# Block attention and two dense layers on one core: token regions ahead of weight forms in SBUF, one attention step on another engine, longer planned zero products, a new order

## The chip, the core and the metric

The kernel runs on one core of a Trainium2 chip. The metric is device time in microseconds (us). Engines: PE (TensorE, matmuls), PEld (its weight loads), DVE (VectorE), ACT (ScalarE), POOL (GpSimd), SP (SyncE, which issues the transfers). Each takes its instructions in the order of the program, and semaphores tie the engines together.

## The reference

Attention inside chunks of 64 tokens (4 batches, 8 heads, 576 tokens, head size 64), then two dense layers on the 2304 x 512 result:

```
scores = scale * (q_c @ k_c.T)            # per chunk of 64
scores = scores - max(scores)
attn = exp(scores) / (sum(exp(scores)) + 1e-09)
x = (attn @ v_c) as 2304 x 512
x = (s * relu(x @ w_in)**2 + b) @ w_out           # 512 -> 2048 -> 512
x = (softplus(x @ moe2_w_in)) @ moe2_w_out        # 512 -> 2048 -> 512
```

All data is float32.

## The kernel before

**Numbers in halves.** Float32 operands are cut into two fp32r parts, `hi` (ACT casts it, L616) and `lo` (DVE subtracts, L625), and each product is three matmuls: hi·hi, hi·lo, lo·hi. The weights come as 64-bit words from DRAM and are turned into floats on the chip by `convert`: per tile of 128x512 DVE runs L483, L499, L514 and L583, and ACT one or two activations.

**Products.** The first matrix of each layer is multiplied by Winograd's form of Strassen's scheme: `quad(ph, i, j)` makes seven products (`p1` to `p7`) for a block of weights `i` (8 of them) and a group of tokens `j` (3 of them), so 24 quads a layer. A product is six matmuls of 128 x 384 columns (two inner halves by three part products, L1073). The products accumulate on one another in PSUM: `p1` is copied by ACT to a second bank (a seed, L1095), `p6` adds to the first, ACT or DVE takes a copy (L438 or L440), `p7` adds again, ACT seeds a third bank and DVE subtracts (L603), and so on. So five or six products of a quad wait for an ACT or DVE instruction that itself waits for an earlier product of the same quad. Other quads' products stand between as the order has them. The second matrix (`second_by_blocks`, matmuls at L1362) runs over 21 steps a layer, each of 8 x 6 matmuls.

**Attention.** Nine units `u` of 256 tokens each. For each: scores on PE (L847), a maximum by DVE (L868, `tensor_reduce`), and for half of the heads (`EARLY`) the maximum times -1/8 by DVE (L891, `tensor_scalar`), eight exponentials by ACT with it as the bias (L879); the other half has its maximum subtracted by DVE (L924) and one exponential (L937). Sums, reciprocals (L957 ACT, L960 DVE), the scaling by POOL (L964), transposes (L978), values (L1005), then the seven Strassen forms of the tokens as hi and lo (`block_forms`).

**Order.** Each step is an `Op` with candidate engines, a key and its dependencies. `Work.order` lays all 3907 of them out by a list schedule over estimated costs; the keys decide among those that are ready, and `TUNE` is a table of offsets to the keys. So the order on each engine is a result of `TUNE` and of the ops' engines. `Work.warmed` then fills the planned idle time of PE in the attention part with zero products (128 x 512 matmuls of zeros into bank S2, L1566), as many as fit by the cost that it plans for one.

**Place in SBUF.** One pool hands out SBUF in the order in which tiles are made: `operands` (two buffers of Strassen weight forms), `mem` (raw weights, sums, staging), small tiles, and then the six `region` tiles (token forms), at their first use. In every quad the weights stand in `operands` and the tokens in two regions. In the second matrices the tokens are hi and lo pieces in region 4 (layer one) or 0 (layer two), and the weights stand in `operands` too, with two exceptions: forms 4 to 7 of layer one stand in regions 1 and 2 (4 x 3 steps of 48 matmuls, 576), and the last eighth of the other steps stands higher up in the tokens' own region (10 x 3 x 6, 180). So of the 4032 matmuls of products 3276 have their weights in `operands` and 756 in a region.

Of the kernel before, what the change touches and what calls it, by code (L numbers as in the profile page):

```python
# [8 lines left out]
F32 = mybir.dt.float32  # L9
F32R = mybir.dt.float32r  # L10
# [3 lines left out]
ALU = mybir.AluOpType  # L14
# [4 lines left out]
P = 128  # L19
# [10 lines left out]
SCALE = 1.0 / float(D) ** 0.5  # L30
# [46 lines left out]

REGION = GROUP * XS // 2
TYPED = {(r, v) for r in range(2 * NG) for v in (1, 3)} | {(1, 2), (2, 2), (4, 2), (0, 4)}
AT_FORMS2 = 0  # L80
LATE = 4
AT_RAWS = 2048, 3 * REGION
# [8 lines left out]
SUMS_BY = ["POOL"] * 2 + ["DVE"] * 6  # L91

TUNE = {
# [36 lines left out]
}  # L130


# [18 lines left out]
class Work:  # L151
# [11 lines left out]
    BYTES = 330e3  # L163

    COLD = 7.0

    def __init__(self):
        self.ops = []
# [103 lines left out]

    def warmed(self, done, emit, kind, index):

        t, out, unused = 0.0, [], True
        for op in done:
            unused = unused and all((u.kind, u.index) != (kind, index) for u in op.takes)
            if op.on == "PE" and unused:
                for x in range(int((op.start - t) / self.IDLE / (2 if op.start < self.COLD else 1))):
                    out.append(Op({"PE": self.IDLE}, 0, [], [], [], emit, 0))  # L280
                    out[-1].on, out[-1].start = "PE", t + x * self.IDLE
                    out[-1].end = out[-1].start + self.IDLE
                t = op.end
            out.append(op)
        return out
# [20 lines left out]
def block_attention_two_layers(  # L306
# [36 lines left out]
    nc = tc and tc.nc  # L343
    work = Work()

    if tc:
        const = ctx.enter_context(tc.tile_pool(name="const", bufs=1))
        dram = ctx.enter_context(tc.tile_pool(name="dram", bufs=1, space=DRAM))
        pp = ctx.enter_context(tc.tile_pool(name="psum", bufs=1, space=PSUM))
        operands = const.tile([P, AT_WF - AT_W1], F32R, name="operands")  # L350
        shared = {}
        plain = const.tile([P, WORDS - AT_WF], F32, name="mem")
        bank = {
            kind: [pp.tile([P, 512], F32, name=f"{kind}{i}") for i in range(n)]
            for kind, n in (("A", 2), ("S", 3), ("at", 3))
        }
        ident = const.tile([P, P], F32, name="ident")
        nought = const.tile([P, P], F32R, name="nought")
        minus = minus_r = None
        s_sb = const.tile([P, 1], F32, name="s_sb")  # L360
        b_sb = const.tile([P, 1], F32, name="b_sb")
        small = [
            [const.tile([P, 2 * H], F32, name=f"{x}{i}") for x in ("mx", "sm")]
            for i in range(2)
        ]
        summed = {
            (ph, n, j): dram.tile([P, NF, N], F32, name=f"summed{ph}_{n}_{j}")
            for ph in range(2)
            for n in range(1, 8)
            for j in range(NG)  # L370
        }
        forms2 = [dram.tile([P, 7, NF, 256], F32, name=f"forms2_{ph}") for ph in range(2)]
        bias = const.tile([P, KK], F32, name="bias")
        unit = const.tile([P, 8], F32, name="unit")
# [415 lines left out]
    held = {}  # L790
# [10 lines left out]
    def attention(u, key):  # L801
# [56 lines left out]
        mx, sm = small[u % 2] if tc else (None,) * 2  # L858
        heads = lambda x: x.rearrange("p (h k) -> p h k", k=D)
        copied = []  # L860
        for hp in range(2):
            sc, pt = scores_in[hp], Place("at")
            h = slice(hp * H, (hp + 1) * H)
# [5 lines left out]
                    out=mx[:, h], in_=heads(at(sc)), op=ALU.max, axis=AX.X  # L869
# [4 lines left out]
            if (u, hp) in EARLY:  # L874

                def exps(e, sc=sc, hp=hp):
                    for y in range(H):
# [8 lines left out]
                        )  # L886

                o3 = add(
                    {"DVE": 0.08},
                    key,  # L890
                    lambda e, h=h: nc.vector.tensor_scalar(  # L891
                        out=mx[:, h], in0=mx[:, h], scalar1=-SCALE, scalar2=None, op0=ALU.mult
                    ),
                    [o2],
                )
                o5 = add({"ACT": 8 * 0.3}, key, exps, [o3], [sc], w=es)
            elif (u, hp) in BY_PE:

                def shift(e, sc=sc, h=h):
# [14 lines left out]
                        out=of("e", hp), in_=at(sc), func=AF.Exp, scale=SCALE  # L914
# [5 lines left out]
            else:  # L920
# [4 lines left out]
                        out=heads(of("e", hp)),  # L925
                        in0=heads(at(sc)),
                        in1=mx[:, h].unsqueeze(2).to_broadcast([P, H, D]),
                        op=ALU.subtract,
# [9 lines left out]
                        out=of("e", hp), in_=of("e", hp), func=AF.Exp, scale=SCALE  # L938
# [4 lines left out]
            if (u, hp) not in EARLY:  # L943
# [3 lines left out]
                    lambda e, h=h, hp=hp: nc.vector.tensor_reduce(  # L947
                        out=sm[:, h], in_=heads(of("e", hp)), op=ALU.add, axis=AX.X
                    ),
                    [o4],  # L950
                    r=es,
# [5 lines left out]
                lambda e, h=h: nc.scalar.activation(out=sm[:, h], in_=sm[:, h], func=AF.Identity, bias=1e-9),  # L957
# [10 lines left out]
                    op=ALU.mult,  # L968
# [667 lines left out]
```

## Time and profile before

| | |
|---|---|
| runs | 815.45 us median of three (812.33 to 816.46) |
| the profiled execution | 815.57 us, of which 813.8 us is the span from the first to the last instruction |
| PE busy | 785.0 us, 96% |
| DVE, ACT, POOL busy | 688.1, 551.2, 151.9 us |
| transfers | 214.94 MB, mean 264 GB/s |
| granted TensorE clock | 0.994 of full on the mean |

The stages, from the timeline: attention mixed with the first quads to about 105 us, the other quads of layer one to about 280 us, its second matrix to about 450 us, the quads of layer two to about 632 us, its second matrix to the end. The page's slices are 20.3 us wide; PE is at "9" or close to it nearly everywhere, so what matters is how many matmuls a stretch holds and what the short gaps wait for.

### The profile page before, as it was taken

To read this page: it belongs to the slowest core of one execution; us is meant where nothing else is said; L and a number is where in the kernel's file an instruction comes from. 1 tells how busy PE (TensorE), PEld (TensorE's weight loads), DVE (VectorE), ACT (ScalarE), POOL (GpSimd) and SP (SyncE) were. 2 spreads that over 40 slices of the span, in tenths; PEclk is the share of its full clock that TensorE was granted. 3 is DMA by queue.
4 is the path that set the end of the run, shared out by engine and by line. 5 is a ranking of instruction groups with operands and counts; after the bars stand their busy time and mean duration, and the time that the engine had idled before them with its cause. 6 is when DMAs were issued, how large, how long until landed. Compare 5 with 4: busy or idle time off the path is not lost.

```text
span 813.8 us, 15584 instructions
## 1 busy us (share of the span) xinstructions
PE 785.0 (96%) x5374; PEld 758.0 (93%) x5374; DVE 688.1 (85%) x1318; ACT 551.2 (68%) x1241; POOL 151.9 (19%) x146
## 2 busy tenths in 40 slices
PE   9998989899899899999999999999999999999998
PEld 6777889899899799999999899999999999999998
DVE  5989877998997779999999899999965867777865
ACT  4678977878987856778687756566555656555543
POOL 1677545121210004000022340121210000000000
PEclk9998999999999999999999999999999999999999
DMA  8656368989989997999862167989979987678851
GB/s 305 215 178 213 116 208 293 316 302 320 358 279 343 360 330 275 351 360 349 291 222 79 39 217 265 309 295 317 331 254 331 314 328 238 226 238 284 284 175 59
DMA packets 99279, 214.94 MB, mean 264 GB/s; under 512 B 10368, under 2 KB 71040, under 8 KB 97664
## 3 DMA queue, kind: packets, MB, share of 16 engines
q1 hardware_dynamic: 99200, 213.95, 76.7%
q8 instruction: 42, 0.69, 0.4%
q14 instruction: 37, 0.30, 0.1%
HBM read 128.45 MB, written 85.46 MB: 263 GB/s over the span
## 4 chain that ended last, share of the span: by engine, by line
PE 58%; DVE 8%; ACT 3%; DMA 2%; issue 1%; POOL 0%; ACTq 0%
PE S L1362 15%; PE at L1362 15%; PE at L1073 11%; PE A L1362 10%; PE S L1073 5%; PE A L1073 3%; DVE mem L603 2%; DVE region L625 2%; DMA summed<-mem 2%; ACT region L616 1%; DVE operands L625 1%; DVE mem L569 0%; DVE mem L514 0%; ACT mem L1105 0%; ACT S L1095 0%
## 5 line engine op out<-in xcount | busy, mean ns | idle before, releaser
L1073 PE MATMUL at<-region,operands 128*128 128x384 f32 x960 | 186.4, 340 | 5.7 <-ACT S L1095 4.6
L603 POOL TENSOR_TENSOR mem<-mem 128x256 f32<-128x256 f32 (+1 forms) x109 | 111.5, 1034 | 390.2 <-DVE mem L583 304.3
L1073 PEld LDWEIGHTS at<-region,operands 128*128 128x128 f32 x960 | 168.9, 188 | 10.6 <-ACT S L1095 8.2
L616 ACT CAST region<-mem 128x384 fp32r<-128x384 f32 (+3 forms) x210 | 110.1, 533 | 71.7 <-PE at L1362 44.8
L625 DVE TENSOR_TENSOR region<-mem,region 128x384 fp32r<-128x384 f32 (+2 forms) x204 | 112.5, 564 | 34.9 <-ACT region L616 33.7
L616 ACT CAST region<-region 128x384 fp32r<-128x384 f32 (+3 forms) x206 | 104.7, 521 | 53.5 <-PE at L1362 38.7
L625 DVE TENSOR_TENSOR region<-region,region 128x384 fp32r<-128x384 f32 (+3 forms) x206 | 113.9, 571 | 23.8 <-ACT region L616 22.5
L603 DVE TENSOR_TENSOR mem<-mem 128x384 f32<-128x384 f32 (+1 forms) x237 | 126.7, 556 | 7.7 <-ACT mem L1105 3.1
L1073 PE MATMUL S<-region,operands 128*128 128x384 f32 x624 | 127.0, 342 | 3.5 <-ACT S L1095 2.9
L1073 PEld LDWEIGHTS S<-region,operands 128*128 128x128 f32 x624 | 111.6, 190 | 6.0 <-ACT S L1095 4.2
L1362 PE MATMUL S<-region,operands 128*128 128x384 f32 (+1 forms) x504 | 116.2, 338 | 0.4 <-DVE region L625 0.4
L1362 PE MATMUL at<-region,operands 128*128 128x384 f32 (+1 forms) x504 | 115.7, 338 | 0.0
L1073 PE MATMUL A<-region,operands 128*128 128x384 f32 x432 | 90.4, 348 | 5.3 <-DVE A L603 2.5
L1362 PEld LDWEIGHTS S<-region,operands 128*128 128x128 f32 x504 | 90.5, 188 | 0.7 <-DVE region L625 0.7
L1362 PEld LDWEIGHTS at<-region,operands 128*128 128x128 f32 x504 | 90.7, 188 | 0.0
L1073 PEld LDWEIGHTS A<-region,operands 128*128 128x128 f32 x432 | 76.9, 191 | 8.4 <-DVE A L603 4.4
L1105 ACT ACTIVATE mem<-S 128x384 f32<-128x384 f32 x104 | 50.6, 490 | 26.2 <-PE S L1073 9.9
L625 DVE TENSOR_TENSOR operands<-mem,operands 128x768 fp32r<-128x768 f32 (+2 forms) x56 | 56.7, 1018 | 2.0 <-ACT operands L616 1.2
L1095 ACT COPY S<-at 128x384 f32<-128x384 f32 x80 | 37.9, 474 | 22.5 <-PE at L1073 19.8
L1116 ACT ACTIVATE mem<-mem 128x384 f32<-128x384 f32 x96 | 49.0, 529 | 1.1
L616 ACT CAST operands<-mem 128x768 fp32r<-128x768 f32 (+2 forms) x56 | 46.2, 834 | 4.7 <-POOL mem L603 3.0
L1362 PE MATMUL S<-region,region 128*128 128x384 f32 x192 | 45.1, 338 | 2.7 <-ACT region L616 1.9
(103 smaller groups left out, 1068.3 us busy)
## 6 DMA issues: line engine op xcount, KB each, us to landing
summed<-mem SPq DMA_DIRECT2D x336, 192.0 KB, 4.2
region<-summed SPq DMA_DIRECT2D x44, 768.0 KB, 5.9
mem<-in_w_dram SPq DMA_DIRECT2D x64, 512.0 KB, 5.2
mem<-summed SPq DMA_DIRECT2D x40, 768.0 KB, 5.0
forms<-mem SPq DMA_DIRECT2D x12, 512.0 KB, 5.3
region<-forms SPq DMA_DIRECT2D x6, 1024.0 KB, 8.4
mem<-forms SPq DMA_DIRECT2D x6, 1024.0 KB, 7.3
region<-in_q_dram SPq DMA_DIRECT2D x18, 256.0 KB, 4.0
```

What stands on the lines that cost most here:

```text
L603: lambda e: on(e).tensor_tensor(out=out(), in0=x(), in1=y(), op=op or ALU.subtract),
L616: lambda e: nc.scalar.copy(out=hi().bitcast(F32R), in_=x()),
L625: lambda e: on(e).tensor_tensor(out=lo().bitcast(F32R), in0=x(), in1=hi(), op=ALU.subtract),
L1073: nc.tensor.matmul(acc(dst)().rearrange("p (u c) -> p u c", u=GROUP), l[a], r[c], start=start and kk == 0 and x == 0, stop=kk == 1 and x == 2,
L1095: lambda e: nc.scalar.copy(out=acc(place)(), in_=acc(ba)()),
L1105: lambda e: nc.scalar.activation(out=at(go), in_=acc(place)(), func=AF.Softplus if ph else AF.Relu),
L1116: lambda e: nc.scalar.activation(out=at(go), in_=at(go), func=AF.Square),
L1362: nc.tensor.matmul(at(accs[d])[:, : N if c else N + more], l[a], r[c], start=i == 0 and y == 0, stop=i == NF - 1 and y == 2,)
```

## The change

Four edits: the six region tiles are made before all others; the negated maximum is made by ACT in place of DVE; `warmed` starts its zero products at 4.2 us of the plan and gives one that begins before 8 us 1.9 times the usual cost (before: from 0, twice the cost if the op after them starts before 7 us); and `TUNE` is another table, which moves instructions on every engine.

```
+FIRST_USES = [(0, 1), (1, 1), (2, 1), (3, 1), (4, 0), (5, 0)]
...
 TUNE = {
-    "attention 0": -425.5, "attention 0/0": -645, "attention 0/16": 5, "attention 1": -590.5,
+    "attention 0": -366, "attention 1": -248, "attention 1/25": 22.5, "attention 1/28": -18,
...
+    FIRST = 4.2
...
-        t, out, unused = 0.0, [], True
+        t, out, unused = self.FIRST, [], True
...
-                for x in range(int((op.start - t) / self.IDLE / (2 if op.start < self.COLD else 1))):
+                while True:
+                    cost = self.IDLE * (1.9 if t < self.COLD + 1 else 1)
+                    if t + cost > op.start:
+                        break
...
+        shared = {
+            (r, v): const.tile([P, REGION], F32R if (r, v) in TYPED else F32, name=f"region{r}_{v}", tag=f"region{r}")
+            for r, v in FIRST_USES
+        }
         operands = const.tile([P, AT_WF - AT_W1], F32R, name="operands")
-        shared = {}
...
-                    {"DVE": 0.08},
+                    {"ACT": 0.12},
                     key,
-                    lambda e, h=h: nc.vector.tensor_scalar(
-                        out=mx[:, h], in0=mx[:, h], scalar1=-SCALE, scalar2=None, op0=ALU.mult
-                    ),
+                    lambda e, h=h: nc.scalar.mul(out=mx[:, h], in_=mx[:, h], mul=-SCALE),
```

Where the tiles lie in each partition, in bytes, as the two built programs have it:

| tile | before | after |
|---|---|---|
| six regions, 21504 each | 99328 to 228352 | 16512 to 145536 |
| `operands`, 28672 | 16512 | 145536 |
| `mem`, 52736 | 45184 | 174208 |

Counted over the whole order, the zero products (L1566 before, L1577 after) are 113 before and 109 after. Of the 144 products of each layer that wait for an ACT or DVE step on their own quad, the number with no other PE step or just one between the product that is read and the one that waits was 33 in layer one and 40 in layer two; now it is 24 and 33. With none between: 4 and 1; now 0 and 2.

DVE at the start of the program. `mx` holds maxima, `sm` sums, `mem` the raw weights of the first block, `at` are PSUM banks with scores. Before:

```order
L868 TENSOR_REDUCE mx_77<-at_70 128x8
L499 TENSOR_SCALAR mem<-mem 128x512
L891 TENSOR_SCALAR mx_77<-mx_77 128x8
L868 TENSOR_REDUCE mx_77<-at_71 128x8
L514 SCALAR_TENSOR_TENSOR mem<-mem 128x512
L924 TENSOR_TENSOR region_0_143<-at_71,mx_77 128x512
```

And now:

```order
L496 TENSOR_SCALAR mem<-mem 128x512
L512 TENSOR_SCALAR mem<-mem 128x512
L527 SCALAR_TENSOR_TENSOR mem<-mem 128x512
L512 TENSOR_SCALAR mem<-mem 128x512
L496 TENSOR_SCALAR mem<-mem 128x512
L527 SCALAR_TENSOR_TENSOR mem<-mem 128x512
L596 SCALAR_TENSOR_TENSOR mem<-mem 128x512 x2
L881 TENSOR_REDUCE mx_83<-at_76 128x8
L881 TENSOR_REDUCE mx_83<-at_77 128x8
```

The eight steps of the first block's conversion have moved ahead of the first maximum (on SP the two transfers that bring it now stand ahead of the first four of q and k, too), and the negation of `mx` is gone from DVE.

On PE, late in the attention part, the end of quad (1, 1) of layer one. Each row is the first of the five that make up a product. Before, `A1` is the bank that the products accumulate in and `S2`, `S0` are the seeded banks:

```order
L1073 MATMUL S1_68<-region2_1_796,operands_63 128x384
...
L1073 MATMUL A1_66<-region2_1_796,operands_63 128x384
...
L1073 MATMUL S2_69<-region2_1_796,operands_63 128x384
...
L1073 MATMUL A1_66<-region2_1_796,operands_63 128x384
...
L1073 MATMUL S0_67<-region2_1_796,operands_63 128x384
```

And now, where `A0` and `S1` belong to quad (0, 1):

```order
L1084 MATMUL A1_72<-region2_1_65,operands_69 128x384
...
L1084 MATMUL S2_75<-region2_1_65,operands_69 128x384
...
L1084 MATMUL A0_71<-region2_1_65,operands_69 128x384
...
L1084 MATMUL S1_74<-region2_1_65,operands_69 128x384
...
L1084 MATMUL S0_73<-region2_1_65,operands_69 128x384
...
L1084 MATMUL A1_72<-region2_1_65,operands_69 128x384
```

Before, the product on a seeded bank follows directly on the `A1` product whose result the seed or the subtraction takes; now three products stand between the first such pair.

## Rows read from the trace of the kernel before

**Rows 1.** The page: span, and busy time of each engine.

```profile
span 813.8 us, 15584 instructions
PE 785.0 (96%) x5374; PEld 758.0 (93%) x5374; DVE 688.1 (85%) x1318; ACT 551.2 (68%) x1241; POOL 151.9 (19%) x146
```

**Rows 2.** Four stretches: length, busy PE, PEld, DVE, ACT, POOL, then PEclk, DMA, GB/s.

```profile
60.00:80.00 20.00, 17.11 (x311) 15.26 (x310) 18.06 (x36) 17.02 (x65) 15.41 (x14) 0.83 0.70 238
100.00:120.00 20.00, 16.50 (x82) 15.53 (x81) 15.76 (x25) 14.11 (x31) 10.27 (x10) 0.91 0.60 202
120.00:280.00 160.00, 150.96 (x831) 144.45 (x830) 137.71 (x266) 131.44 (x279) 29.79 (x29) 1.00 0.94 322
620.00:780.00 160.00, 160.00 (x913) 160.00 (x912) 118.88 (x224) 93.33 (x188) 0.00 (x0) 1.00 0.82 278
```

**Rows 3.** Waits of PE's weight loads, 120 to 640 us: total, times, longest.

```profile
PEld at L1073 <- ACT S L1095: 8.2, 11, 2.5
PEld A L1073 <- DVE A L603: 4.4, 5, 2.0
PEld S L1073 <- ACT S L1095: 3.1, 3, 1.5
```

**Rows 4.** Timeline, 0 to 10 us: start, length, engine, line, operation.

```profile
2.59 0.91 SPq L446 DMA_DIRECT2D mem<-in_w_dram  x2
4.24 3.97 PE L1566 MATMUL S<-nought 128*128 128x512 f32 x9
8.15 0.69 PE L847 MATMUL at<-region 64*64 64x64 f32 x32
9.95 0.69 DVE L868 TENSOR_REDUCE mx<-at 128x8 f32<-128x512 f32 x1 [7.92 <-PE at L847]
```

**Rows 5.** DMA issues: bytes and median time to landing.

```profile
mem<-in_w_dram SPq DMA_DIRECT2D x64, 512.0 KB, 5.2
```

**Rows 6.** Groups of DVE's instructions by line: busy, mean ns, idle before.

```profile
L514 DVE SCALAR_TENSOR_TENSOR mem<-mem 128x512 f32<-128x512 uint32 x56 | 38.5, 698 | 0.1
L483 DVE TENSOR_SCALAR mem<-mem 128x512 int32<-128x512 int32 x64 | 27.6, 432 | 6.5 <-DMA mem<-in_w_dram 6.5
L891 DVE TENSOR_SCALAR mx<-mx 128x8 f32<-128x8 f32 x9 | 8.1, 895 | 0.0
```

**Rows 7.** Line L891: shortest, median, longest in ns; and who waited.

```profile
L891 DVE TENSOR_SCALAR mx<-mx x9: 161/755/2152, 10.9 to 84.8; 128x8 f32<-128x8 f32 x9
  ACT region L879: 18.4, 7
```

**Rows 8.** Timeline, 66 to 76 us: POOL, DVE and PE around one L891.

```profile
66.95 2.59 POOL L625 TENSOR_TENSOR region<-mem,region 128x1024 fp32r<-128x1024 f32 x1 [0.40 <-ACT region L616]
68.40 1.17 DVE L891 TENSOR_SCALAR mx<-mx 128x8 f32<-128x8 f32 x1
72.14 0.33 PE L847 MATMUL at<-region 64*64 64x64 f32 x2 [0.76 <-ACT region L879]
```

**Rows 9.** Line L957, ACT on a tile of the same size: shortest, median, longest.

```profile
L957 ACT ACTIVATE sm<-sm x18: 205/253/294, 14.0 to 89.5; 128x8 f32<-128x8 f32 x18
```

**Rows 10.** Zero products, group of PE's instructions: busy, mean ns.

```profile
L1566 PE MATMUL S<-nought 128*128 128x512 f32 x113 | 32.5, 425 | 0.0
```

**Rows 11.** Groups of matmuls, 372 to 398 us: busy, mean ns, idle.

```profile
L1362 PE MATMUL at<-region,region 128*128 128x384 f32 x66 | 15.0, 334 | 0.0
```

**Rows 12.** The same, 690 to 716 us.

```profile
L1362 PE MATMUL at<-region,operands 128*128 128x384 f32 x45 | 10.5, 337 | 0.0
```

**Rows 13.** The chain that ended last, pieces of 48 matmuls: start, length.

```profile
367.12 8.32 PE A L1362 x48
658.68 8.43 PE A L1362 x48
```

**Rows 14.** Two groups of matmuls by their operands, whole span.

```profile
L1073 PE MATMUL at<-region,operands 128*128 128x384 f32 x960 | 186.4, 340 | 5.7 <-ACT S L1095 4.6 <-ACT mem L438 1.0
L1362 PE MATMUL at<-region,operands 128*128 128x384 f32 (+1 forms) x504 | 115.7, 338 | 0.0
```

More of the change, by code (lines that the diff above doesn't have):

```diff
@@ L278, in warmed @@
             if op.on == "PE" and unused:
-                for x in range(int((op.start - t) / self.IDLE / (2 if op.start < self.COLD else 1))):
+                while True:
+                    cost = self.IDLE * (1.9 if t < self.COLD + 1 else 1)
+                    if t + cost > op.start:
+                        break
                     out.append(Op({"PE": self.IDLE}, 0, [], [], [], emit, 0))
-                    out[-1].on, out[-1].start = "PE", t + x * self.IDLE
-                    out[-1].end = out[-1].start + self.IDLE
+                    out[-1].on, out[-1].start, out[-1].end = "PE", t, t + cost
+                    t += cost
                 t = op.end
```

75 rows, old and new, of the table TUNE are left out of this document.

## The prediction

> **What bounds the kernel now.** I read the page first: PE is busy 785.0 of 813.8 us [rows 1], so PE is the bound on the whole and only three things can move the time: how many matmuls there are, how long one takes, and how long PE stands still. The windows tell where it stands still. From 620 to 780 us PE runs 913 matmuls in 160 us with no idle time, 0.1752 us each: the pace when nothing waits. From 120 to 280 us it runs 831 in the same length [rows 2]; the 82 that are missing are 14.4 us. The view of waits says for what: after 120 us its three largest entries are weight loads of the quads that wait for ACT's seeds (L1095) and DVE's subtractions (L603), 8.2 + 4.4 + 3.1 = 15.7 us in 19 waits [rows 3].
>
> The attention part has two breaks of another sort. In 60 to 80 us PE is idle 2.89 us and the granted clock is 0.83 on the mean, in 100 to 120 us idle 3.50 us at 0.91 [rows 2]: part of each stretch ran at 1.2 GHz in place of 2.4 after PE had stood still. Counted as time lost that is 2.89 + 3.50 + 0.17 x 20 + 0.09 x 20 = 11.6 us. In 60 to 80 us DVE is busy 18.06 of 20 us and ACT 17.02; both engines are nearly full where PE waits for them.
>
> The start is late. PE runs nine zero products from 4.24 to 8.2 us and only then the first scores, and DVE has nothing to do until 9.95 us, since its first maximum needs these scores and the conversion of the first weights stands behind it [rows 4].
>
> **The change, part by part.**
>
> *Zero products.* 113 become 109. In all they keep PE busy 32.5 us [rows 10], 0.29 us each with overlap counted once, so four fewer give at most 1.2 us; I take -0.9, as the ones at the start run into each other least. The new start at 4.2 us of the plan is where PE in fact begins (4.24, [rows 4]), so the plan no longer counts on zeros before that.
>
> *The first weights.* Their two transfers are issued from 2.59 us now [rows 4] and go ahead of q and k. A weight transfer lands 5.2 us after its issue [rows 5], so DVE can start its conversion near 6 us in place of 9.95. Eight DVE steps move into that hole: four at about 0.43 and four at about 0.70 us [rows 6], 4.5 us. What it costs: the first scores come two issues later (0.91 us, [rows 4]), and PE has zeros to run meanwhile.
>
> *The negation.* On DVE it should be a trifle, and its shortest takes 161 ns, but the median is 755 and the longest 2152 [rows 7]; nine take 8.1 us [rows 6]. Rows 8 show why: POOL runs one instruction from 66.95 to 69.54 us, and the negation that starts at 68.40 ends at 69.57, with POOL's. ACT stands idle 18.4 us before its exponentials because of this line, 7 of 9 times [rows 7], and at 72.14 us PE waits for the bank that those exponentials free [rows 8]; the break with the lower clock follows. On ACT the nearest row is L957 on a tile of the same size, 253 ns [rows 9], so nine cost ACT 2.3 us and DVE saves 8.1. ACT's negation waits for DVE's maximum at the head of ACT's queue; behind it are the eight exponentials, which wait for it anyway, and after them the casts and seeds. Nothing that is not waiting today comes to stand behind a new wait.
>
> Together DVE has 12.6 us less to do before the last token form is ready. PE gains less: its zero products are fixed in the order, so only the two breaks can close, at most 11.6 us and at least nothing. ACT gets 2.3 us more in a part in which it is already busy 17.02 of 20 us [rows 2], and what DVE no longer holds up, ACT will. I take a quarter: -2.9.
>
> *The new order among the quads.* Here I count places, not times. Products that wait for an ACT or DVE step on their own quad with no or one PE step between: 33 + 40 before, 24 + 33 now, 78%. If the 15.7 us of waits [rows 3] go with that count, 3.4 us go away. Bounds: if each reordered quad brings a new wait elsewhere, +3; if the four with nothing between in layer one carried twice their share, -8. I take -3.4.
>
> *The place in SBUF.* Matmuls of the same shape with no idle time take 334 ns when their weights are in a region and 337 when they are in `operands` [rows 11, 12]. A step of 48 matmuls runs 8.32 us in the first case and 8.43 in the second, where 42 of the 48 have weights in `operands` [rows 13]: 0.11 / 42 = 2.6 ns each. The largest groups of both code lines, all with weights in `operands`, stand at 340 ns, waits of the quads included, and 338 [rows 14]; by the layout 3276 matmuls are slow and 756 fast. What sets the two apart? Two properties go together in every case of before: weights in a region lie above the tokens that they meet, weights in `operands` below; and regions begin at a multiple of 512 bytes, `operands` 128 bytes behind one. After the change `operands` lies above all tokens. By the first property 3276 matmuls become fast (-8.5 us) and the 576 whose weights lie in regions 1 and 2, now below region 4, slow (+1.5): -7.0. By the second, if both sides must begin alike, all become fast: -8.5; if only the distance to a multiple of 512 counts, the 756 become slow: +2.0. The first two make it likelier than not. About half of layer one's 1008 quad matmuls stand where PE waits anyway, 1008 x 2.6 / 2 = 1.3 us, so of -7.0 I take -5.7. Copies and subtractions touch the same tiles from both layouts, and I cost the move at nothing for them: DVE has 160 - 118.88 us free in 620 to 780 us to hide it [rows 2].
>
> The Trainium skill speaks against a gain here: the page "SBUF — State Buffer", section "SBUF: two separate sides", says that PE never waits on anyone for SBUF and has two read ports that are independent of each other, and gives no weight to the place of a tile. By that page the move is worth 0 and the sum below is 5.7 us less. The 334 against 337 ns here is not explained by it.
>
> **The sum**, against the profiled execution's 815.57 us (the median of three is 815.45, the same): -0.9 - 2.9 - 3.4 - 5.7 = -12.9, which gives 802.7 us. Of that, 12.9 is 1.6%; about 0.5% (4 us) can be told from no change in this kernel.
>
> **The rivals.**
>
> A. *The place does not matter* (or `operands` itself is slow for a reason that moves with it). For it: only two classes of weights were seen. Against it: the classes differ in every step that holds both, as in the one of rows 13. Then 815.57 - 7.2 = 808.4.
>
> B. *The waits only move.* ACT takes DVE's part in 0 to 120 us, and among the quads the longer distances bring as many waits as the short ones lose. For it: ACT's 17.02 of 20 us, and DVE's 137.71 of 160 in 120 to 280 us [rows 2]. Then only zeros and place are left: 815.57 - 0.9 - 5.7 = 809; with half the place, 812.
>
> C. *Slower: ACT is the bound of the attention part.* Each of its late seeds and exponentials stops PE, and a stop like those of 60 to 80 us costs 2.89 idle + 3.4 at the lower clock = 6.3 us [rows 2]. It decides from two more such breaks than now, with nothing gained in waits: 815.57 - 0.9 - 5.7 + 12.6 = 821.6; with the place at nothing one more is enough to be above 820.
>
> D. *Gains that cancel*: the alignment reading (+2.0) and new waits (+3) against zeros and the start: 815 to 817.
>
> **How the numbers follow.** Forecast 0.50 (798 to 807), A 0.20 (804 to 812), B 0.14 (806 to 814), D 0.08, C 0.08. The range leaves out C and part of D on the upper side and, below, the case that both breaks close and the place gives 8.5 (815.57 - 0.9 - 11.6 - 3.4 - 8.5 = 791): 795 to 815. Faster by over 0.5% (below 811.4): 0.50 + 0.19 + 0.09 = 0.78; within 0.5%: 0.01 + 0.05 + 0.07 + 0.01 = 0.14; slower: 0.07 + 0.01 = 0.08.
>
> **What would show it.** Right: the maximum's negation on ACT near 0.25 us, nine times; DVE's first conversion near 6 us; granted clock near 1.00 in 60 to 80 us; more than 831 matmuls in 120 to 280 us; weights in `operands` at 334 ns and 48 matmuls in 8.32 us at the end of the kernel, and, if it is the side on which the weights lie, 337 ns for forms 4 to 7 of layer one's second matrix. Wrong: 337 ns as before in layer two (A, and the time is then near 808), ACT's idle time before the exponentials as long as now with DVE's maximum as its cause (B), or new stretches of lower clock (C).

## The result and the profile after

The changed kernel takes 803.17 us (median of four runs, 801.67 to 804.17) against 814.68 us for the kernel before, run beside it on the same chip. The quotient of the two medians is 0.9859, 11.5 us; the ratio on record, with its interval, is 0.9835 (95%: 0.9806 to 0.9865). Run a second time beside another set of runs of the kernel before, it gave 0.9858 (0.9831 to 0.9885). Both values are used below where they differ. The forecast was 802.7 us.

The page of the changed kernel, as [rows 1]:

```profile
span 802.4 us, 15623 instructions
PE 775.6 (97%) x5370; PEld 751.4 (94%) x5370; DVE 682.6 (85%) x1314; ACT 553.0 (69%) x1245; POOL 148.9 (19%) x146
```

Its windows, as [rows 2], with one more from 80 to 100 us; the last one is taken 10 us earlier, since the kernel is ahead by then:

```profile
60.00:80.00 20.00, 19.00 (x396) 16.74 (x394) 18.27 (x36) 19.72 (x69) 15.12 (x13) 1.00 0.38 131
80.00:100.00 20.00, 16.77 (x150) 15.13 (x150) 16.41 (x29) 12.69 (x27) 12.83 (x15) 1.00 0.46 161
100.00:120.00 20.00, 14.96 (x70) 14.27 (x71) 14.33 (x24) 13.36 (x28) 8.36 (x9) 0.88 0.68 232
120.00:280.00 160.00, 153.61 (x850) 148.77 (x849) 140.89 (x269) 134.61 (x285) 29.60 (x28) 0.98 0.95 327
610.00:770.00 160.00, 160.00 (x924) 159.77 (x923) 118.74 (x226) 93.26 (x189) 0.00 (x0) 1.00 0.83 284
```

and the kernel before from 80 to 100 us:

```profile
80.00:100.00 20.00, 19.84 (x350) 18.43 (x349) 17.23 (x34) 19.08 (x60) 12.57 (x13) 1.00 0.32 108
```

In a stretch where PE never stands still it now runs 924 matmuls, against 913. The break in 60 to 80 us is gone (PE idle 1.00 us, clock 1.00). But PE now stands idle 3.23 us in 80 to 100 us, where it was 0.16 us, and 5.04 us at a clock of 0.88 in 100 to 120 us, where it was 3.50 at 0.91. These windows no longer hold the same work, for the attention part ends 11 us earlier. The last matmuls of that part, those with the values, before and after (behind the three durations stand the first and the last start):

```profile
L1005 PE MATMUL at<-region x576: 218/218/268, 20.3 to 95.3; 64*64 64x64 f32 x192
```

```profile
L1016 PE MATMUL at<-region x576: 218/218/267, 19.8 to 84.2; 64*64 64x64 f32 x192
```

The pace, from the groups of matmuls in 680 to 706 us (layer two, weights in `operands`), as [rows 12]:

```profile
L1373 PE MATMUL at<-region,operands 128*128 128x384 f32 x47 | 10.7, 334 | 0.0
```

from the groups in 366 to 392 us (layer one, weights in regions 1 and 2), as [rows 11]:

```profile
L1373 PE MATMUL at<-region,region 128*128 128x384 f32 x66 | 15.0, 334 | 0.0
```

and from the chain that ended last, as [rows 13]:

```profile
649.08 8.32 PE A L1373 x48
```

Both places now run at 334 ns, and a step of layer two's second matrix takes 8.32 us where it took 8.43.

The start, from the timeline, as [rows 4]:

```profile
4.58 0.43 DVE L496 TENSOR_SCALAR mem<-mem 128x512 int32<-128x512 int32 x1 [2.56 <-DMA mem<-in_w_dram]
7.78 0.69 PE L860 MATMUL at<-region 64*64 64x64 f32 x32 [0.99 <-DMA region<-in_k_dram]
10.05 1.29 DVE L881 TENSOR_REDUCE mx<-at 128x8 f32<-128x512 f32 x2 [0.56 <-PE at L860]
```

DVE begins the conversion at 4.58 us, earlier than the forecast 6, and is through with its eight steps when the first maximum can start at 10.05 us (9.95 before). The negation, now on ACT, as [rows 7]:

```profile
L904 ACT ACTIVATE mx<-mx x9: 203/209/234, 10.8 to 73.4; 128x8 f32<-128x8 f32 x9
  DVE mx L881: 0.4, 1
```

ACT stood idle 18.4 us before its exponentials; now it is idle 0.4 us before the negation, and not at all before the exponentials. The waits of the quads' weight loads, 120 to 640 us, as [rows 3]:

```profile
PEld at L1084 <- ACT S L1106: 6.4, 6, 2.6
...
PEld S L1084 <- ACT S L1106: 2.4, 2, 1.5
...
PEld A L1084 <- DVE A L616: 1.6, 6, 0.4
```

These are 10.4 us in place of 15.7, but that is not a gain: the view begins at 120 us, and the quads' waits have moved ahead of this edge. This entry is from 85 to 125 us:

```profile
PEld A L1084 <- ACT S L1106: 7.1, 4, 3.6
```

From 80 to 640 us all entries of the quads' weight loads add up to 23.0 us before and 22.4 us now. What counts in the end is PE's idle time right before the quads' matmuls. Of the kernel before (its third group, on `at`, with 5.7 us, stands in [rows 14]):

```profile
L1073 PE MATMUL S<-region,operands 128*128 128x384 f32 x624 | 127.0, 342 | 3.5 <-ACT S L1095 2.9 <-DVE S L603 0.7
L1073 PE MATMUL A<-region,operands 128*128 128x384 f32 x432 | 90.4, 348 | 5.3 <-DVE A L603 2.5 <-ACT S L1095 2.4
```

and now:

```profile
L1084 PE MATMUL at<-region,operands 128*128 128x384 f32 x960 | 181.8, 336 | 4.8 <-ACT S L1106 4.5 <-DVE mem L616 0.3
L1084 PE MATMUL S<-region,operands 128*128 128x384 f32 x624 | 126.2, 340 | 4.9 <-DVE S L616 3.2 <-ACT S L1106 1.8
L1084 PE MATMUL A<-region,operands 128*128 128x384 f32 x432 | 89.2, 344 | 6.4 <-ACT S L1106 6.0 <-ACT mem L1116 0.3
```

That is 14.5 us before and 16.1 us now: among the quads PE stands still as long as it did.

### The profile page after: what moved, and what is told of

It is laid out like the page before. It is cut to its first block, busy times and chain, and to the rows that moved or that the text cites. A ratio compares the mean times of both kernels' runs of the same rounds, so it can differ in the third digit from the quotient of the medians.

```text
span 802.4 us, 15623 instructions
## 1 busy us (share of the span) xinstructions
PE 775.6 (97%) x5370; PEld 751.4 (94%) x5370; DVE 682.6 (85%) x1314; ACT 553.0 (69%) x1245; POOL 148.9 (19%) x146
## 4 chain that ended last, share of the span: by engine, by line
PE 73%; DVE 9%; ACT 6%; DMA 5%; issue 3%; POOL 3%; SPq 0%; DVEq 0%; POOLq 0%; ACTq 0%
PE S L1373 16%; PE at L1373 16%; PE at L1084 14%; PE A L1373 9%; PE S L1084 8%; PE A L1084 5%; PE S L1577 3%; POOL mem L616 2%; DVE mem L616 2%; DMA summed<-mem 2%; DVE region L638 2%; DMA mem<-in_w_dram 1%; ACT operands L629 1%; ACT mem L1116 1%; ACT mem L1127 1%
## 5 line engine op out<-in xcount | busy, mean ns | idle before, releaser
L1084 PE MATMUL at<-region,operands 128*128 128x384 f32 x960 | 181.8, 336 | 4.8 <-ACT S L1106 4.5
L616 POOL TENSOR_TENSOR mem<-mem 128x256 f32<-128x256 f32 (+1 forms) x109 | 109.3, 1016 | 391.6 <-DVE mem L596 285.7
L1084 PEld LDWEIGHTS A<-region,operands 128*128 128x128 f32 x432 | 75.3, 190 | 10.4 <-ACT S L1106 7.6
```

What stands on the lines that cost most here:

```text
L616: lambda e: on(e).tensor_tensor(out=out(), in0=x(), in1=y(), op=op or ALU.subtract),
L1084: nc.tensor.matmul(acc(dst)().rearrange("p (u c) -> p u c", u=GROUP), l[a], r[c], start=start and kk == 0 and x == 0, stop=kk == 1 and x == 2,
```

## The experiments

Each kernel below differs from one of the two by what its diff shows; "..." marks lines left out. Ratios are to the kernel before, run beside it on the same chip, with 95% intervals; 0.001 is 0.8 us. The kernel before had medians of 817.54, 815.13 and 816.82 us beside the three sets of runs, so absolute times of different sets can't be compared to a microsecond, and the expectations, which are in absolute times, have to be read with the ratio beside them. In the expectations, 173.3 and 176 ns a matmul are the paces of 48 in 8.32 and in about 8.45 us.

**What makes a matmul fast.** Theory "side": a matmul is fast when its weights lie above its tokens. Theory "alike": it is fast when both begin at the same distance from a multiple of 512 bytes. The rival "nothing": place does not matter.

The layout alone, on the kernel before:

```
+FIRST_USES = [(0, 1), (1, 1), (2, 1), (3, 1), (4, 0), (5, 0)]
...
+        shared = {
+            (r, v): const.tile([P, REGION], F32R if (r, v) in TYPED else F32, name=f"region{r}_{v}", tag=f"region{r}")
+            for r, v in FIRST_USES
+        }
         operands = const.tile([P, AT_WF - AT_W1], F32R, name="operands")
-        shared = {}
```

> The kernel before with one edit, the regions made first (its order, its negation on DVE and its zero products stay). Theory 'alike' (a product matmul is fast when its weights and its tokens begin at the same distance from a multiple of 512 bytes) and theory 'side' (fast when the weights lie above the tokens): weights in operands at 334 ns in place of 337, layer two's second matrix at 173.3 ns a matmul, 807 to 809 us. Rival 'nothing' (the place does nothing, the faster matmuls come with the new order): 337 ns and 813 to 816 us.

0.9934 (0.9910 to 0.9958), 812.52 us beside 817.54. Its groups in 680 to 706 us:

```profile
L1366 PE MATMUL at<-region,operands 128*128 128x384 f32 x47 | 10.7, 334 | 0.0
```

So "nothing" is refuted. Next, a small empty tile is made ahead of the regions, with the order of the tiles as before:

```
         unit = const.tile([P, 8], F32, name="unit")
+        gap = const.tile([P, 32], F32, name="gap")
```

> The kernel before with one empty tile of 128 bytes per partition ahead of the regions: operands still lies below all regions, but regions and operands now both begin 128 bytes behind a multiple of 512. 'Alike': 334 ns for weights in operands, 807 to 809 us, as with the whole move. 'Side': 337 ns and 813 to 816 us, as before.

0.9937 (0.9916 to 0.9957). Same view:

```profile
L1363 PE MATMUL at<-region,operands 128*128 128x384 f32 x46 | 10.5, 334 | 0.0
```

128 empty bytes do what the whole move does, with `operands` still below all regions, so "side" is refuted. The counter-test on the changed kernel:

```
+        gap = const.tile([P, 32], F32, name="gap")
         operands = const.tile([P, AT_WF - AT_W1], F32R, name="operands")
```

> The changed kernel with one empty tile of 128 bytes between the regions and operands: operands still lies above all regions, but begins 256 bytes behind a multiple of 512 and the regions 128. 'Alike': 337 ns for weights in operands (and still 334 for weights in regions), 809 to 811 us. 'Side': 334 ns, 802 to 804 us.

0.9884 (0.9863 to 0.9905), 808.92 us. Same view:

```profile
L1374 PE MATMUL at<-region,operands 128*128 128x384 f32 x45 | 10.5, 338 | 0.0
```

With `operands` above all tokens but 128 bytes apart from them (in their distance from a multiple of 512), the matmuls are slow again. The same edit with 64 floats in place of 32, one execution:

> The changed kernel with an empty tile of 256 bytes between the regions and operands, so that they begin 256 bytes apart in their distance from a multiple of 512. If what counts is that they begin alike within 512 bytes: 176 ns a matmul for weights in operands, as with 128. If the unit is 256 bytes: 173.3 ns, as in the changed kernel.

804.83 us, and in the same view:

```profile
L1374 PE MATMUL at<-region,operands 128*128 128x384 f32 x46 | 10.5, 334 | 0.0
```

And with 16 floats, one execution:

> The changed kernel with an empty tile of 64 bytes between the regions and operands, so that they begin 64 bytes apart in their distance from a multiple of 256. If only equal distances within 256 bytes are fast: 175 to 176 ns a matmul for weights in operands. If the unit is 64 bytes or less: 173.3 ns.

810.26 us, and:

```profile
L1374 PE MATMUL at<-region,operands 128*128 128x384 f32 x45 | 10.4, 338 | 0.0
```

So 0 and 256 bytes apart are fast, 64 and 128 slow: what counts is the distance within 256 bytes, as far as these four distances tell. Others were not tried. It is the distance between the two and not the place of one: `operands` begins 128 bytes behind a multiple of 512 in the kernel before, where it is slow, and in the changed kernel, where it is fast.

Taking the layout back from the changed kernel (the diff of the first experiment, reversed):

> The changed kernel with the layout of before (order, negation and zero products as changed). Both 'alike' and 'side': 337 ns for weights in operands, 809 to 811 us, so that order, negation and zeros are worth 4 to 5 us and the layout 6 to 8. 'Nothing': 334 ns and 803 us.

0.9884 (0.9863 to 0.9905), 808.56 us. Same view:

```profile
L1370 PE MATMUL at<-region,operands 128*128 128x384 f32 x45 | 10.3, 338 | 0.0
```

The pace is as expected, the shares are not. By the ratios order, negation and zeros together are worth 9.5 us here, not 4 to 5, and the layout on top of them 2.1 to 4.0 us (by the two ratios of the changed kernel), not 6 to 8.

**What the negation is worth.** On the kernel before, the operation alone is issued on ACT, and the plan is told nothing of it, so all other instructions keep their places:

```
-                    lambda e, h=h: nc.vector.tensor_scalar(
-                        out=mx[:, h], in0=mx[:, h], scalar1=-SCALE, scalar2=None, op0=ALU.mult
-                    ),
+                    lambda e, h=h: nc.scalar.mul(out=mx[:, h], in_=mx[:, h], mul=-SCALE),
```

> The kernel before, with the negation of the maxima issued on ACT at the same place of the order; every other instruction stands where it stood. Theory 'DVE held': the nine negations take 0.25 us each on ACT, DVE is 5 to 8 us less busy before 90 us, the break with the lower clock in 60 to 80 us closes at least in part, and the time falls by 2 to 5 us (0.994 to 0.998 of before). Rival 'only moved': PE's order with its zero products holds, another wait takes the place, 0.998 to 1.002.

0.9947 (0.9924 to 0.9970). What the line itself waits for:

```profile
L891 ACT ACTIVATE mx<-mx x9: 193/209/213, 10.2 to 82.4; 128x8 f32<-128x8 f32 x9
  DVE mx L868: 8.8, 2
```

So of ACT's 18.4 us of idle time 8.8 stay in this order: there ACT waits for the maximum itself. Two of its windows (20 to 60 us, 60 to 80 us):

```profile
20.00:60.00 40.00, 38.86 (x719) 31.90 (x716) 35.25 (x69) 30.55 (x111) 28.09 (x23) 1.00 0.66 214
60.00:80.00 20.00, 17.01 (x311) 15.16 (x310) 17.05 (x33) 17.37 (x63) 16.07 (x14) 0.83 0.61 205
```

and the kernel before in the first of these windows:

```profile
20.00:60.00 40.00, 36.78 (x648) 29.65 (x647) 36.04 (x69) 27.74 (x99) 27.99 (x24) 1.00 0.59 193
```

The gain is not where it was forecast. PE's idle time in 20 to 60 us falls from 3.22 to 1.14 us. What falls is the wait of the value matmuls' weight loads for a copy on DVE in these 40 us, before and now:

```profile
PEld at L1005 <- DVE region L440: 4.6, 4, 2.1
```

```profile
PEld at L1003 <- DVE region L440: 1.6, 4, 0.6
```

The break in 60 to 80 us, with its clock of 0.83, stands as before. Its longest wait is not for the exponentials but for a subtraction on DVE, before and now:

```profile
74.12 1.98 PE L847 MATMUL at<-region 64*64 64x64 f32 x62 [1.67 <-DVE mem L603]
```

```profile
70.56 1.15 PE L847 MATMUL at<-region 64*64 64x64 f32 x62 [2.00 <-DVE mem L603]
```

The attention part ends 3.0 us earlier:

```profile
L1003 PE MATMUL at<-region x576: 218/218/267, 19.8 to 92.3; 64*64 64x64 f32 x192
```

The profiled execution is the slowest of its nine, 814.68 us against a median of 811.44; its granted clock in 120 to 280 us is 0.98 where the kernel before has 1.00, about 3 us by our estimate (0.02 x 160), and so its span is only 0.9 us shorter.

The reverse, on the changed kernel (the same diff, turned round):

> The changed kernel, with the negation issued on DVE again at the same place of the order. 'DVE held': its median is well above 0.2 us, ACT's idle time before the exponentials is back, and the time rises by 2 to 6 us against the changed kernel (805 to 809 us, 0.987 to 0.992 of before). 'Only moved': 802 to 804 us, 0.983 to 0.985.

0.9927 (0.9901 to 0.9953), 810.4 us: more than the range that was expected. By the ratios the negation is worth 5.6 to 7.5 us in the new order. The attention part ends 7 us later than in the changed kernel:

```profile
L1018 PE MATMUL at<-region x576: 218/218/267, 20.4 to 91.4; 64*64 64x64 f32 x192
```

The group on DVE:

```profile
L904 DVE TENSOR_SCALAR mx<-mx 128x8 f32<-128x8 f32 x9 | 9.1, 1014 | 0.0
```

and what the exponentials, L892, waited for:

```profile
  DVE mx L904: 11.6, 8
```

In another order the nine cost DVE 9.1 us, where it was 8.1. One of them, beside POOL's instruction:

```profile
57.24 2.38 POOL L638 TENSOR_TENSOR region<-mem,region 128x1024 fp32r<-128x1024 f32 x1
57.89 1.75 DVE L904 TENSOR_SCALAR mx<-mx 128x8 f32<-128x8 f32 x1
```

POOL ends at 59.62 us, the negation at 59.64. So do seven of the nine here and six of the nine in the kernel before: each begins while POOL runs and ends with POOL's instruction. The other five, with POOL idle, take 0.16 or 0.17 us. But with the negation on DVE the break in 60 to 80 us is closed too:

```profile
60.00:80.00 20.00, 18.21 (x388) 16.07 (x389) 18.34 (x40) 18.10 (x64) 10.59 (x10) 1.00 0.45 155
```

So it is the new order that closes it.

**What the zero products are worth.** The old `warmed` in the changed kernel:

```
-        t, out, unused = self.FIRST, [], True
+        t, out, unused = 0.0, [], True
...
-                while True:
-                    cost = self.IDLE * (1.9 if t < self.COLD + 1 else 1)
...
+                for x in range(int((op.start - t) / self.IDLE / (2 if op.start < self.COLD else 1))):
...
```

> The changed kernel with the old rule for the zero products: 135 in place of 109, as the plan of the changed order has more idle time than its rule now fills. If PE's own stream is the bound of the attention part, 26 more at 0.23 us (the first ones 0.43) cost 5 to 8 us: 808 to 811 us, 0.990 to 0.993 of before. If DVE and ACT bound it, they stand in time that is idle anyway: 802 to 805 us.

0.9913 (0.9891 to 0.9936), 808.98 us, 4.5 to 6.4 us above the changed kernel by the two ratios of the latter. The group of the zero products, with this rule and in the changed kernel:

```profile
L1574 PE MATMUL S<-nought 128*128 128x512 f32 x135 | 37.4, 417 | 0.0
```

```profile
L1577 PE MATMUL S<-nought 128*128 128x512 f32 x109 | 31.0, 418 | 0.0
```

They keep PE busy 6.4 us longer, and most or all of that is paid. The other way, fewer:

```
-    IDLE = 0.22
+    IDLE = 0.26
```

> The changed kernel with 0.26 us planned for a zero product in place of 0.22: 92 of them in place of 109. If PE's own stream bounds the attention part, 17 fewer at 0.23 us save 3 to 4 us: 0.995 to 0.997 of the changed kernel. If DVE and ACT bound it, 0.999 to 1.001. If PE's longer idle stretches bring the lower clock into the attention part, 1.002 or more, with a granted clock below 1.00 before 60 us.

0.9849 (0.9818 to 0.9880), 803.25 us beside 803.86 for the changed kernel: no difference. Its window of 20 to 40 us, and the changed kernel's:

```profile
20.00:40.00 20.00, 16.68 (x298) 12.88 (x296) 16.44 (x32) 14.52 (x55) 9.19 (x9) 0.91 0.62 210
```

```profile
20.00:40.00 20.00, 20.00 (x390) 15.94 (x386) 17.42 (x38) 18.12 (x74) 12.54 (x11) 1.00 0.76 255
```

With 17 fewer, PE is idle 3.32 us in this window and the granted clock falls to 0.91. With all of them, PE is never idle there. That idle time and the lower clock take back what is saved in zeros is how we read the equal times; which of them weighs more is not shown.

**What the order is worth alone.** The changed kernel with the layout of before and the negation on DVE, that is both reversed diffs together:

> The changed kernel with the layout of before and the negation issued on DVE: the new order and the new rule for zero products alone. By the terms of the prediction (fewer zeros -0.9, shorter waits among the quads -3.4, part of the breaks): 809 to 812 us, 0.993 to 0.996 of before. Rival 'the order pays only with the other two edits': what the runs with one edit taken back cost, added up (7 for the negation, 4 to 5 for the layout), gives 814 to 816 us, 0.998 to 1.002.

0.9979 (0.9961 to 0.9997), 814.37 us. The gain is small and only just clear of noise, below the range that the prediction's terms gave and at the edge of the rival's.

**The changed kernel again**, beside the last three:

> The changed kernel itself, as the measure for the others on this chip: 0.981 to 0.987 of before, and no theory differs on it.

0.9858 (0.9831 to 0.9885). Its profiled execution has a span of 796.8 us, 5.6 less than the first one's, and these windows:

```profile
60.00:80.00 20.00, 19.31 (x396) 17.08 (x396) 18.59 (x37) 19.72 (x69) 15.12 (x13) 1.00 0.37 126
100.00:120.00 20.00, 14.59 (x72) 13.90 (x72) 14.27 (x25) 13.91 (x28) 8.24 (x8) 0.91 0.67 233
120.00:280.00 160.00, 154.37 (x868) 149.38 (x867) 143.70 (x274) 135.02 (x287) 30.23 (x29) 1.00 0.97 334
```

The same program: 868 matmuls in 120 to 280 us at a clock of 1.00, against 850 at 0.98.

**Do the three edits add up?** Layout 0.9934, negation 0.9947 and order with zeros 0.9979, each alone, give 0.9861 multiplied, against 0.9858 and 0.9835 measured for all three. But the pairs do not all follow. Order and negation together (the run with the layout taken back) are at 0.9884 where the product is 0.9926, about 3 us better and outside that run's interval (0.9863 to 0.9905), though the product has an interval as wide. The negation is worth 4.3 us in the old order and 5.6 to 7.5 us in the new one, and the layout 5.4 us alone, 4.2 us on top of the order, and 2.1 to 4.0 us on top of order and negation. So the agreement of the whole does not fix the parts, and part of the order's worth comes only with the negation on ACT.

## Why the prediction was right

The time was forecast within about a microsecond. Two of the four terms have a cause that the runs bear out, the place and the negation; the one for the order among the quads did not come, and the negation's larger worth stands in for it. That the sum fits so closely is luck. Term by term:

**The place, forecast -5.7: right in size, wrong in its reason.** Alone it is worth 5.4 us (0.0066 of 815; interval 3.4 to 7.3). The 2.6 ns were read correctly from [rows 11 to 13]: all groups come to 334 ns. But the sum took the reading by sides, -7.0 before the deduction, under which the 576 matmuls of regions 1 and 2 would have become slow. They stayed at 334 ns, and 128 empty bytes made the slow ones fast with the sides as they were. The reading that holds is the one that the text gave -8.5, in a unit of 256 bytes. With it the deduction of 1.3 us for layer one's quads leaves 7.2, more than any of the measures of the layout (2.1 to 5.4 us), though their intervals are some 2 us wide to either side: the deduction was likely too small, and the two errors met. The rule that PE never waits on anyone (the Trainium skill, "SBUF — State Buffer", "SBUF: two separate sides") would have given 0; the trace differs, 338 against 334 ns for the same instructions with 128 bytes between two tiles as the only edit.

**The negation and the first weights, forecast -2.9 by way of the two breaks: mis-sized, and the place was wrong.** The negation alone is worth 4.3 us (interval 2.4 to 6.2), more than the whole term. On ACT it takes 209 ns, near the row of the same size (253). But "only the two breaks can close" was wrong: it gives its time back in 20 to 60 us, where the prediction had not looked for idle time. The break in 60 to 80 us does not close by it. There the prediction read the wait of 0.76 us for the exponentials; right behind it stands the longer one of 1.67 us for DVE's L603, which the negation leaves as it is. The break closes by the new order, with the negation on either engine, while PE's idle time in 80 to 120 us grows from 3.66 to 8.27 us. Whether ACT has become the bound of the attention part is open: it is busy 19.72 of 20 us in 60 to 80 us, and PE idle only 1.00. DVE's early start is there (4.58 us), and the first scores lose nothing (7.78 against 8.15 us); its own share was not measured by a run of its own. Its 4.5 us were counted among what DVE has less to do, but these steps are only earlier, not gone.

**The zeros, forecast -0.9, and the order among the quads, -3.4: too large together, and the second has no wait behind it.** Order and zeros alone give 1.7 us (interval 0.2 to 3.2). The count of short distances fell to 78% as the prediction says, but the waits did not go with it: PE's idle time before the quads' matmuls is 14.5 us before and 16.1 us now (15.3 in the second profile, 15.7 with the order alone). The 15.7 us that the term was taken from left out the waits ahead of 120 us, where the first quads already run, and they were set beside 14.4 us that are missing in 120 to 280 us, where PE is idle only 9.04. What the new order did shorten is the attention part, and mostly together with the negation: its last matmuls start at 95.3 us before, at 91.4 in the new order with the negation on DVE, and at 84.2 with it on ACT. Of the zeros, 17 fewer changed nothing and 26 more cost 4.5 to 6.4 us; the four fewer than before were not measured by a run of their own.

**Rivals.** A (the place does nothing), the slower case C and D (gains that cancel) are refuted by the times. Of B ("the waits only move") the half on the quads is what the profile shows; its forecast of 809 us failed because the attention part gained. In sum, -12.9 was forecast and -11.5 measured by the medians (-13.4 by the ratio beside them), with the layout near its term or below it, the negation above, the order below.

## What to carry to other kernels

Compare the mean time of one instruction over all its places before looking at waits: 3 ns in 337, the same wherever the weights came from one tile, were worth about as much as moving the negation, and an empty tile of 128 bytes gets them. A tiny operation can be dearer than a large one: the 128 x 8 negation took 895 ns on the mean where a step of 128 x 512 took 698 [rows 6], so look at the spread from shortest to longest (161 to 2152 ns) and at what another engine runs when it is long. When a change moves a stage in time, windows at fixed times hold other work than before; add up waits over the whole stage. A forecast summed from several terms can be right while half of them are off, so measure the edits one by one, and in pairs: here they multiply to the whole and still depend on one another.

## What was not expected of the hardware

A matmul's pace depends on how far apart its two SBUF operands begin within 256 bytes: 334 ns at 0 and 256 bytes, 338 at 64 and 128. A step of 48 tells what that means for the pace: 8.32 us when alike, 8.43 us in the kernel before. It stays 334 ns whether the weights lie above or below the tokens. Why is not known; only these four distances and one shape were tried.

The same program gave spans of 802.4 and 796.8 us in two executions, with a mean granted clock of 0.991 and 0.997. Over these spans the clock alone makes 4.8 of the 5.6 us, by our estimate (0.009 x 802.4 less 0.003 x 796.8). The first has granted clocks of 0.88 and 0.98 in 100 to 120 us and in 120 to 280 us where the second has 0.91 and 1.00; PE had been idle 5.04 and 5.41 us in the first of these stretches. So a single profile of this kernel is good to about 0.7%.
